# A ring of four places, and the tensor engine's steady state as a loop of two heads: one decode step of gated attention and SwiGLU

## The chip, the core and the metric

The kernel runs on one core of a Trainium2 chip. The metric is device time in microseconds (us) from the start of the program to its end. The kernel before takes 2550.09 us (median of 3 runs, 2549.92 to 2551.15).

The engines have short names in the profile: PE is the tensor engine (PEld its weight loads), DVE the vector engine, ACT the scalar engine, POOL the general engine, and SP the engine that only issues DMAs here. An engine's name with a q behind it (SPq) is its sequencer: it waits or issues while the engine itself computes nothing.

## What is computed

One token `x` (1 x 512) is mixed from an attention branch and an MLP branch:

```python
# H, Sk, Dh = 32, 65536, 128; all inputs bf16
g = sigmoid((x * gate_w).sum())
q = (x @ wq).reshape(H, Dh)
scores = einsum("hd,hkd->hk", q, k_cache) * Dh ** -0.5
o = einsum("hk,hkd->hd", softmax(scores), v_cache)
a = o.reshape(H * Dh) @ wo
b = (silu(x @ w_gate) * (x @ w_up)) @ w_down        # w_gate, w_up: 512 x 1792
out = g * a + (1 - g) * b
```

Each head has 16 MB of keys and 16 MB of values, so the two caches together are 1.07 GB that are read once. Everything else is small: `wq` and `wo` are 4 MB each, the three MLP weights 1.75 MB each.

## The kernel before

**Stream.** SP issues all large reads in one fixed order, made by `plan_stream` (L25 to L50). A read brings 32 KB to each of the 128 partitions, 4 MB in all; a head has four reads of keys and four of values, written here K(h,t) and V(h,t). The order is: `wq`, K(0,0), `wg`, `wu`, `wd`, then the rest of the keys of heads 0 and 1, and from head 2 on K(h,t) and V(h-2,t) by turns. Values trail keys by two heads, and the last eight reads are values, with `wo` ahead of the last head's. The very last read is cut into pieces of 2, 1 and 1 MB.

**Ring.** The reads land in `ring`, 160 KB per partition, as 20 slots of 8 KB (L78 to L97). A normal read takes four slots, so there are five places. `wq` has the first, K(0,0) the second, `wg` and `wu` share the third, `wd` has the fourth with a gap behind it, and K(0,1) the fifth. Before a read is issued SP waits until the former owner of its slots is used up (L219 to L229): `s_q` for `wq` (the query projection has run), `s_h` for `wg` and `wu` (the MLP's first products have run), `s_b` for `wd`, `ktdone` for keys (transposed by DVE), `pvdone` for values (multiplied by PE). SP issues in order, so a wait also holds back all later reads.

**Keys.** DVE transposes a place of keys in two units of 2 MB into `kt`, which has two buffers (L361 to L367, `kt[:, i % 2]`); the second waits for PE to have finished with the unit two before (`qkdone`). PE then runs 16 matmuls of 512 columns per unit (L459), which lay the scores of a head over one bank of PSUM, `psS`. After a head's eighth unit DVE takes the maximum, POOL reduces it over the partitions, ACT takes the exponential with a running sum, and DVE turns the probabilities into `pb`.

**Values.** PE multiplies a place of values in four half units (L473 to L482), 32 matmuls of 512 columns in all, into `psO`. ACT scales a finished head by the inverse of its sum (`row_norm`), and PE's `turn` (L428) transposes the row with 4 small matmuls into a column of `psT`. Head 31 is done otherwise: 128 matmuls of one column per place (L485). When the second place of head 31 is done, PE waits for `wo` and runs `project` for heads 0 to 30 (L492 to L495), 31 matmuls of 512 columns; `project(31)` follows after the last values. DVE casts the 31 columns of `psT` at once before that (L380).

**MLP.** It is folded into the start. PE runs `mlp_up` after the fourth unit of keys of head 0 (the second half of K(0,1)) and `mlp_down` after the fifth. On DVE `mlp_steps` stands behind the transpose of the fifth unit.

PE's whole program is written out, 9118 matmuls with 9118 weight loads.

## Time and profile before

| what | value |
|---|---|
| median of 3 runs | 2550.09 us |
| profiled execution | 2550.52 us |
| its span (first to last instruction) | 2548.7 us |
| mean granted clock of PE | 0.917 |
| read from HBM | 1087.64 MB, 427 GB/s over the span |
| busy: PE, DVE, ACT, POOL | 2052.2, 1168.9, 54.4, 25.9 us |
| one transpose of a key unit (L367) | 4426 ns |
| 4 MB of keys or values, from issue to landing (median) | 37.8 and 39.7 us |

The span is 1.8 us shorter than the time of the same execution; that rest lies ahead of and behind the program's instructions. Busy times are of one profiled execution. Matmuls are pipelined and their ends are modelled, so PE's busy share says little by itself. The time from issue to landing holds the wait behind the reads issued earlier, since all share one queue. A line number in the profile is a line of the kernel before.

### The profile page before, as it was taken

How to read it: one execution, taken by the hardware profiler on the slowest of the kernel's cores; microseconds unless marked ns; L12 is line 12 of the kernel's file. 1: busy time of each engine (PE TensorE's matmuls, PEld its weight loads, DVE VectorE, ACT ScalarE, POOL GpSimd, SP SyncE). 2: the span in 40 equal slices, each digit the busy share in tenths (PEclk: the TensorE clock that was granted, in tenths of full speed). 3: DMA queues.
4: the chain of work that ended last, by engine and by line, in shares of the span. 5: the costliest groups of instructions: out<-in, count | busy, mean ns of one | idle time of the engine just before them, and what ended most of it. 6: DMA issues, size and time to landing. Idle time of an engine off the chain costs nothing.

```text
span 2548.7 us, 19566 instructions
## 1 busy us (share of the span) xinstructions
PE 2052.2 (81%) x9118; PEld 812.3 (32%) x9118; DVE 1168.9 (46%) x374; ACT 54.4 (2%) x162; POOL 25.9 (1%) x75
## 2 busy tenths in 40 slices
PE   3888788878888888788778878887888888878886
PEld 2333233333333333233333333332333333333333
DVE  4754544454444444544454444445444544454420
ACT  0000000000000000000000000000000000000000
POOL 0000000000000000000000000000000000000000
PEclk8899999999998999998999998999999899899896
DMA  9999999999999999999999999999999999999998
GB/s 415 401 429 433 430 431 431 432 430 432 428 434 430 434 429 432 430 432 430 431 430 432 430 432 430 432 431 430 432 430 433 429 433 430 431 431 431 432 424 330
DMA packets 41927, 1088.90 MB, mean 427 GB/s; under 512 B 4211, under 2 KB 8310, under 8 KB 8310
## 3 DMA queue, kind: packets, MB, share of 16 engines
q1 hardware_dynamic: 41844, 1087.65, 99.4%
q8 instruction: 71, 1.16, 0.2%
q14 instruction: 10, 0.08, 0.0%
q10 hardware_dynamic: 2, 0.00, 0.0%
HBM read 1087.64 MB, written 0.00 MB: 427 GB/s over the span
## 4 chain that ended last, share of the span: by engine, by line
DMA 59%; PE 27%; DVE 10%; issue 3%; SPq 0%; DVEq 0%
DMA ring<-in_A_k_cache_dram 57%; PE psS L459 13%; PE psO L478 13%; DVE kt L367 10%; DMA ring<-in_A_v_cache_dram 3%; PE psO L485 0%; PE psY L439 0%; PE psT L433 0%; PE psM L416 0%; DVE mxs L349 0%; PE psY L424 0%; SPq L240 0%; DVE brow L345 0%; DVE gwrow L386 0%; DVE pb L355 0%
## 5 line engine op out<-in xcount | busy, mean ns | idle before, releaser
L367 DVE STREAM_TRANSPOSE kt<-ring 128x4096 uint32<-128x4096 uint32 x256 | 1125.4, 4426 | 1254.7 <-DMA ring<-in_A_k_cache_dram 1251.6
L459 PE MATMUL psS<-kt,qw 128*128 128x512 bf16 x4096 | 1110.2, 433 | 453.4 <-DVE kt L367 453.4
L478 PE MATMUL psO<-ring,pb 128*4 128x512 bf16 x3968 | 883.7, 380 | 7.0 <-DMA ring<-in_A_v_cache_dram 7.0
L459 PEld LDWEIGHTS psS<-kt,qw 128*128 128x128 bf16 x4096 | 419.6, 106 | 1142.0 <-DVE kt L367 537.6
L478 PEld LDWEIGHTS psO<-ring,pb 128*4 128x4 bf16 x3968 | 333.3, 87 | 535.3 <-issue 56.3
L290 ACT ACTIVATE nbias<-amx 128x1 f32<-128x1 f32 x32 | 6.5, 203 | 2338.7 <-POOL amx L261 2338.7
L261 POOL PARTITION_ALL_REDUCE amx<-mxs x32 | 11.3, 353 | 2384.5 <-DVE mxs L349 2384.5
L433 PEld LDWEIGHTS psT<-unit,orow 4*128 4x128 f32 x248 | 30.7, 190 | 13.1 <-issue 13.0
L433 PE MATMUL psT<-unit,orow 4*128 4x1 f32 x248 | 33.3, 251 | 0.0
L485 PE MATMUL psO<-pb,ring 128*128 128x1 bf16 x512 | 14.2, 165 | 19.2 <-DMA ring<-in_A_v_cache_dram 18.2
L380 DVE CAST oTn<-psT 128x31 bf16<-128x31 f32 x1 | 0.2, 195 | 61.8 <-PE psT L433 61.8
L355 DVE STREAM_TRANSPOSE pb<-pa 128x512 bf16<-128x512 bf16 x32 | 21.4, 670 | 6.4 <-PE psO L478 6.4
L349 DVE TENSOR_REDUCE mxs<-psS 128x1 f32<-128x512 f32 x32 | 20.9, 653 | 4.8 <-PE psS L459 4.8
L294 ACT ACTIVATE pa<-psS,nbias 128x512 bf16<-128x512 f32 x32 | 22.0, 687 | 1.0
L275 ACT ACTIVATE orow<-psO,Li 4x512 f32<-4x512 f32 x31 | 20.9, 674 | 42.3 <-PE psO L478 37.4
L485 PEld LDWEIGHTS psO<-pb,ring 128*128 128x128 bf16 x512 | 13.9, 102 | 20.2 <-issue 14.1
L263 POOL PARTITION_ALL_REDUCE Lt<-rsum x32 | 12.3, 386 | 36.4 <-ACT pa L294 36.4
L395 PE MATMUL psM<-ones,xrow 1*128 1x1 bf16 x4 | 0.3, 173 | 13.2 <-DMA gwrow<-in_gate_w_dram 13.2
L439 PE MATMUL psY<-ring,oTn 128*1 128x512 bf16 x32 | 10.0, 480 | 0.4 <-DVE oTn L383 0.4
L383 DVE TENSOR_SCALAR oTn<-psO,Li 128x1 bf16<-128x1 f32 x1 | 0.2, 221 | 19.7 <-PE psO L485 19.7
L280 ACT COPY qw<-qd 128x16 bf16<-128x16 bf16 x32 | 7.9, 252 | 6.0 <-DVE qd L333 6.0
L416 PEld LDWEIGHTS psM<-xTb,ring 128*128 128x128 bf16 x112 | 6.9, 159 | 0.2
(39 smaller groups left out, 42.8 us busy)
## 6 DMA issues: line engine op xcount, KB each, us to landing
ring<-in_A_k_cache_dram SPq DMA_DIRECT2D x128, 4096.0 KB, 37.8
ring<-in_A_v_cache_dram SPq DMA_DIRECT2D x127, 4096.0 KB, 39.7
ring<-in_A_wq_dram SPq DMA_DIRECT2D x1, 4096.0 KB, 12.2
ring<-in_A_wo_dram SPq DMA_DIRECT2D x1, 4096.0 KB, 40.3
ring<-in_A_v_cache_dram SPq DMA_DIRECT2D x1, 2048.0 KB, 38.8
ring<-in_A_v_cache_dram SPq DMA_DIRECT2D x2, 1024.0 KB, 40.0
ring<-in_B_w_gate_dram SPq DMA_DIRECT2D x1, 1792.0 KB, 26.2
ring<-in_B_w_up_dram SPq DMA_DIRECT2D x1, 1792.0 KB, 30.0
```

The lines of the kernel that those rows point to most:

```text
L261: nc.gpsimd.partition_all_reduce(amx[:, h:h + 1], mxs[:, h:h + 1], P, RMAX).then_inc(s_ar, 1)
L263: nc.gpsimd.partition_all_reduce(Lt[:, h:h + 1], rsum[:, h:h + 1], P, RADD).then_inc(s_L, 1)
L275: nc.scalar.mul(orow[0:4, :], psO[0:4, h % 2, :], Li[0:4, h:h + 1]).then_inc(s_or, 1)
L294: nc.scalar.activation(pa[:, h % 2, :], psS[:, h % 2, :], ACT.Exp, bias=nbias[:, h:h + 1], scale=SCALE, accum_out=rsum[:, h:h + 1]).then_i ...
L349: nc.vector.reduce_max(mxs[:, h:h + 1], psS[:, h % 2, :], AX_X).then_inc(s_mx, 1)
L355: nc.vector.transpose(pb[:, h % 2, :], pa[:, h % 2, :]).then_inc(s_pb, 1)
L367: nc.vector.transpose(o, src).then_inc(ktdone, 1)
L433: last = nc.tensor.matmul(psT[:, h:h + 1], orow[0:4, i * Dh:(i + 1) * Dh], unit[0:4, i:i + 1], start=(i == 0), stop=(i == 3))
L439: last = nc.tensor.matmul(psY[0:1, :], oTn[:, h:h + 1], wo_ap[:, h, :], start=(h == 0), stop=(h == H - 1))
L459: last = nc.tensor.matmul(psS[:, h % 2, :], qw[:, h % 2, je, at0:at0 + 128], ktb[i % 2][:, je // 2, k, :, je % 2], start=(u == 0 and k == ...
L478: last = nc.tensor.matmul(psO[0:4, h % 2, :], pbk[:, h % 2, col // 16, col % 16:col % 16 + 4], vt[:, r * Dh:(r + 4) * Dh], start=(col == 0 ...
L485: last = nc.tensor.matmul(psO[:, h % 2, 0:1], vt[:, r * Dh:(r + 1) * Dh], pbk[:, h % 2, col // 16, col % 16:col % 16 + 1], start=(col == 0 ...
```

## The change

PE's program, the ring and the place of `wo` are rewritten; the arithmetic and the order of the matmuls of the steady state stay.

- The ring has four places of 32 KB per partition instead of five. Item n of the stream always goes to place n mod 4, so the 16 reads of two heads meet the same addresses in every round.
- `wo` leaves the ring. It is read into `kt`, the two buffers of transposed keys, after the values of head 30, once all matmuls on keys are done.
- On PE the steady state becomes a loop. Ahead of it stand the first 20 items written out; the loop's body holds 16 items (two heads); `(240 - 20) // 16` gives 13 rounds; the last 12 items are written out again. Inside the loop every wait compares a semaphore with a constant plus the loop's register `more`, which grows by 16 a round. So that each semaphore grows by 16 a round, several steps now add `STEP = 8`.
- `turn` uses two columns of `psT` by turns instead of one per head, and so ACT copies each head's column into `oTn` (`column`), and `turn` waits for the copy two heads before. DVE's cast of all columns goes.
- `turn` moves from behind the first quarter of a head's second place of values to its end. `project` for heads 0 to 30 moves from behind the second place of head 31 to behind the third. A place of values is waited for once instead of four times.

```diff
-RING = 20
+NPL = 4
+STEP = 8
...
+    for n, item in enumerate(items):
+        s = n % NPL
...
+        owner[s] = item
+        if item == ("v", H - 2, PL - 1):
+            landed["wo"] = len(dmas)
+            dmas.append((("wo",), 0, 0, None, None))
...
-        ring = sb("ring", [P, RING * HU], BF16)
+        ring = sb("ring", [P, NPL, PLACE], BF16)
...
+        wo_ap = kt[:].rearrange("p b t -> p (b t)").bitcast(BF16).rearrange("p (h n) -> p h n", h=H)
...
+            for n, (item, r0, r1, s, old) in enumerate(dmas):
+                name = item[0]
+                if old is not None and r0 == 0:
+                    if old[0] == "k":
+                        sp.wait_ge(ktdone, 2 * (old[1] * PL + old[2]) + 2)
+                    elif old[0] == "v":
+                        sp.wait_ge(pvdone, old[1] * PL + old[2] + 1)
                     else:
-                        need[key[0]] = 1
+                        sp.wait_ge({"wq": s_q, "wg": s_h, "wd": s_b}[old[0]], 1)
...
+                elif name == "wo":
+                    sp.wait_ge(qkdone, UN * H)
...
+            def column(h):
+                act.wait_ge(s_pt, h + 1)
+                nc.scalar.copy(oTn[:, h:h + 1], psT[:, h % 2:h % 2 + 1]).then_inc(s_oc, STEP)
...
+            def turn(h, more=0):
+                pe.wait_ge(s_or, STEP * (h + 1) + more)
+                if h >= 2:
+                    pe.wait_ge(s_oc, STEP * (h - 1) + more)
...
+            def run(item, more=0):
+                kind, h, t = item
+                if kind == "k":
+                    scores(h, t, more)
+                else:
+                    values(h, t, more)
+                    if t == 1 and h >= 1:
+                        turn(h - 1, more)
...
+            head, per = 4 + 4 * PL, 4 * PL
+            loops = (len(steady) - head) // per
+            for item in first:
+                if item[0] == "k":
+                    run(item)
+            for item in steady[:head]:
+                run(item)
+            with pe.Fori(0, STEP * 2 * loops, STEP * 2) as more:
+                for item in steady[head:head + per]:
+                    run(item, more)
+            for item in steady[head + per * loops:]:
+                run(item)
+            for item in last:
+                run(item)
+                if item == ("v", H - 1, PL - 2):
+                    arrived(pe, landed["wo"])
+                    for h in range(H - 1):
+                        project(h)
             project(H - 1)
```

## Prediction

> **What bounds it now.** I read the page first (DMA row, queues, chain, costliest groups), then SP's own issues in time, then the stages by windows, then PE's last 40 us.

> ```profile
> DMA  9999999999999999999999999999999999999998
> ...
> q1 hardware_dynamic: 41844, 1087.65, 99.4%
> q8 instruction: 71, 1.16, 0.2%
> ...
> DMA 59%; PE 27%; DVE 10%; issue 3%; SPq 0%; DVEq 0%
> ...
> L367 DVE STREAM_TRANSPOSE kt<-ring 128x4096 uint32<-128x4096 uint32 x256 | 1125.4, 4426 | 1254.7 <-DMA ring<-in_A_k_cache_dram 1251.6
> L459 PE MATMUL psS<-kt,qw 128*128 128x512 bf16 x4096 | 1110.2, 433 | 453.4 <-DVE kt L367 453.4
> ```

> The 16 DMA engines are full in all slices, DVE idles for keys, and PE idles for DVE. So the time is bytes at a fixed rate, plus stretches in which the engines have nothing queued, plus what follows the last byte. In the steady state two key transposes start like this:

> ```profile
> 1271.96 8.77 DVE L367 STREAM_TRANSPOSE kt<-ring 128x4096 uint32<-128x4096 uint32 x2 [10.66 <-DMA ring<-in_A_k_cache_dram]
> 1291.39 4.45 DVE L367 STREAM_TRANSPOSE kt<-ring 128x4096 uint32<-128x4096 uint32 x1 [10.66 <-DMA ring<-in_A_k_cache_dram]
> ```

> Both start on a landing, and between them lie one read of keys and one of values: 19.43 us, so 9.71 us for each 4 MB. One stretch of nothing queued shows in the windows of the start (columns: stretch, length, PE, PEld, DVE, ACT, POOL busy, clock, DMA share, GB/s):

> ```profile
> 60.00:64.00 4.00, 4.00 (x65) 3.79 (x63) 1.45 (x1) 0.00 (x0) 0.00 (x0) 1.00 0.95 406
> 64.00:66.00 2.00, 2.00 (x36) 2.00 (x36) 0.00 (x0) 0.00 (x0) 0.00 (x0) 0.87 0.04 16
> 66.00:68.00 2.00, 2.00 (x23) 1.44 (x23) 0.50 (x3) 0.18 (x1) 0.00 (x0) 0.50 0.00 0
> 68.00:72.00 4.00, 4.00 (x11) 1.32 (x10) 0.26 (x2) 0.00 (x0) 0.00 (x0) 0.50 1.09 393
> ```

> SP's waits (us in total, times, longest) and its issue, from the timeline:

> ```profile
> SPq L229 <- PE psM L416: 33.9, 1, 33.9
> ```

> ```profile
> 67.27 0.33 SPq L240 DMA_DIRECT2D ring<-in_A_k_cache_dram  x1
> ```

> The read issued at 67.27 is K(1,0). It waited 33.9 us for `s_h`, since it takes the place of `wg` and `wu`; the reads ahead of it were through near 66 and the queue stood empty about 2.5 us. The end:

> ```profile
> 2522.76 1.01 PE L485 MATMUL psO<-pb,ring 128*128 128x1 bf16 x32 [6.07 <-DMA ring<-in_A_v_cache_dram]
> ...
> 2525.49 2.72 PE L485 MATMUL psO<-pb,ring 128*128 128x1 bf16 x96
> 2528.14 9.39 PE L439 MATMUL psY<-ring,oTn 128*1 128x512 bf16 x31
> 2537.47 4.21 PE L485 MATMUL psO<-pb,ring 128*128 128x1 bf16 x159
> 2542.68 2.75 PE L485 MATMUL psO<-pb,ring 128*128 128x1 bf16 x97 [0.99 <-issue]
> ```

> V(31,1) lands at 2522.7. Two more reads at 9.71 put V(31,2) near 2532.5 and the last piece near 2542.3 (the windows show the engines run dry there). PE ends at 2545.43, the span 3.3 us later.

> **Part 1, the ring at the start: +9.7.** With four places `wq`, K(0,0), `wg`+`wu` and `wd` hold all of them, and each later read shifts one owner back. K(0,1) now waits for `s_q` (17.8, when SP issued K(0,2) before), K(0,2) for K(0,0)'s transposes (32.9): both come while earlier reads still run, so they cost nothing; uncovered they would cost 18 and 33 us. K(0,3), issued before at 32.96, now takes the place of `wg`+`wu` and waits for `s_h`. That can't come earlier: `mlp_up` stands behind the second half of K(0,1), which lands at 46.75 in both. So K(0,3) goes out at 67.27, when K(1,0) did, and every read behind it lands one read later. The queue runs dry at 66 - 9.7 = 56.3 and stands until 68.2: 12 us instead of 2.5. The next wait, K(1,0)'s for `s_b`, ends at 76.42, as K(1,1)'s did before, about 1 us ahead of the end of K(0,3)'s bytes (68.2 + 9.7). DVE and PE lose nothing, because unit 6 of the keys, the first half of K(0,3), is transposed only at 81.7, held up by `mlp_steps`. But nothing gives the DMA time back: **+9.71**, bounds 9.4 and 10.

> **Part 2, the ring in the steady state: 0.** A place of values lands at 1281.67 (1271.96 + 9.71), PE is done with it at 1292.45 (1285.38 + 7.07), and SP's next read goes out at 1292.49: 10.8 us after the landing, 12 where `turn` lies between. Keys take 8.8 (two transposes). With four places three reads, 29.1 us, are still queued at a landing, so 17 us of slack cover the release; with five it was 27. If that cover were gone each us would count.

> **Part 3, the loop's back-edge: 0 on the path, 13 times.** It falls between a `turn` and a K item, where PE idles 3.65 us for DVE. No branch is in the trace; bounds for the stall are 1.0 us (the one idle for "issue", 2542) and 12 us (the 1 KB read of `x`, issued at 1.15 behind a full queue, was waited for until 13.18). Even 12 leaves PE 8.4 late, inside 17. I take 0; the visible stall is the nearer row. [...]

> **Part 4, waits on a register: 0.** The body has 36 (16 `ktdone`, 8 arrivals, 12 others). PE idles for DVE 406.1 us in 140 to 2400, 28 us per round of 16 reads (155.4 us). At the largest regular "issue" gap between weight loads, 0.44 us, 36 cost 16: covered. At nothing, the dropped value waits are a small gain, off the path as well.

> **Part 5, instruction reads: +1.8.** 71 packets for 18311 PE records make 256 instructions each, and 0.2% of the span is 5.1 us, 0.07 a packet. They come all along the run, one per 36 us. A body is 8 x 128 + 32 + 36 to 72, so 4.3 packets. If it stays loaded, 12 x 4.3 packets go: -3.6. If each round reads it anew with two cut or unused blocks, 26 come on top: +1.8. The stall of 0.99 in PE's densest stretch says that little is held ahead, so I take +1.8; doubled traffic, +5.1, is the upper end.

> **Part 6, the end: +3.85.** `project` for 31 heads moves behind V(31,2). Let L be the last landing (2542.5 at most; PE's end is L + 2.93). V(31,2) lands at L - 9.8; its 128 matmuls take 3.55 (row at 2513.14), `project` 9.39, the last place's 128 another 3.5: L + 6.8 with three 0.05 steps, 3.85 later than now. The pieces land during `project`, so PE, not DMA, sets the end. All instructions of `project` count; nothing else is queued behind it but the last values. The 9.39 is 11 matmuls at 0.43 (granted clock 0.50 until 2532) and 20 at 0.21. Bounds: all 31 fast, 6.6, gives +1.0; another stall of 1 us +4.9. [...] The row shows it slow, so I keep 9.39.

> **Without weight.** `wo` in `kt` is gated by matmuls on keys (done at 2456), while SP reaches it behind V(30,3) at 2463: 0; if that wait ended last, V(31,0) and all behind would be late. ACT's 31 copies at 0.25 us lie in an engine 2% busy, wanted two heads on; uncovered 7.8 us. `turn`'s later place and its wait for a copy one head old hold up only values behind it: 0. DVE's dropped cast: 0.

> **Sum.** Profiled execution 2550.52 + 9.71 + 3.85 + 1.8 = 2565.9. The median of the runs is 0.4 lower: **2565.5**.

> **Rivals.** (a) *PE becomes the bound*: 36 waits and one branch cost over 28 us a round, that is 0.78 us per wait. For it: no register wait is in the trace. Against: 0.44 is the largest such gap. At 1 us each, 8 x 13 = 104 us more: 2670. (b) *Not slower: reads get faster.* With three to four reads outstanding instead of four to five, 4 MB might take less than 9.71. From 9.65 on, 256 reads give 15.4 us back and the time is 2550 or less. Against: the engines are at share 1.00 and 431 GB/s in both 140:1200 and 1200:2400, and a queue only needs to be non-empty. (c) *The loop spares its reads and the end runs warm*: 9.4 + 1.0 - 3.6, about 2557, still slower.

> **Chances.** Forecast with its bounds 0.82; (a) 0.07; (b) 0.05; (c) 0.06. Lower bound 2557 from (c); upper 2572 from 10 + 4.9 + 5.1 = 20 above 2550.09, plus 2 for late places after a back-edge; (a) and (b) lie outside. A measurement of this kernel can tell 0.2%, 5.1 us, from no change: slower needs 2555.2. Case (b) is split between same 0.03 and faster 0.02; the rest is slower, 0.95.

> **What would show it.** Right: DMA share near 0 from 56 to 68, SP's `s_h` wait ending with a read at 67.3 that is the eighth large one instead of the ninth; 9.71 us per read after; L439 x31 starting behind V(31,2), and last byte to span's end 9.5 to 11 us instead of 6.3; q8 at 80 to 110 packets. Wrong: PE idling for "issue" by tens of us a round, a DMA share below 0.99 in the middle, or another duration per read.

## The result and the profile after

The changed kernel takes 2555.00 us (median of 20 runs, 2553.04 to 2556.97); the kernel before takes 2550.55 us (20 runs, 2549.56 to 2551.66) in the same comparison. The ratio is 1.0018, with a 95% interval of 1.0011 to 1.0025: slower by 4.5 us, just under the 0.2% that the prediction put as its bound for "slower". The forecast of 2565.5 us is 10.5 us too high, and its range, 2557 to 2572, misses the time by 2 us. The profiled execution took 2555.05 us, its span 2553.3.

The page of the changed kernel, the rows that answer to those shown before:

```profile
DMA  8999999999999999999999999999999999999998
...
q1 hardware_dynamic: 41844, 1087.65, 99.2%
q8 instruction: 22, 0.36, 0.1%
...
DMA 75%; DVE 12%; issue 10%; PE 2%; SPq 0%; DVEq 0%
...
L326 DVE STREAM_TRANSPOSE kt<-ring 128x4096 uint32<-128x4096 uint32 x256 | 1125.6, 4426 | 1255.5 <-DMA ring<-in_A_k_cache_dram 1252.6
L396 PE MATMUL psS<-kt,qw 128*128 128x512 bf16 x3970 | 1104.3, 442 | 463.8 <-DVE kt L326 463.2
```

The first slice of the DMA row has lost a tenth; the rest is as full as before. The instruction queue q8 has 22 packets where it had 71. PE's idle time for DVE is 463 us, as good as the 453 before (some matmul records are missing in this trace).

The start, by windows of the changed kernel (columns as before: PE, PEld, DVE, ACT, POOL busy, clock, DMA share, GB/s):

```profile
52.00:56.00 4.00, 4.00 (x14) 1.49 (x13) 3.14 (x1) 0.00 (x0) 0.00 (x0) 0.69 0.44 188
56.00:60.00 4.00, 3.94 (x22) 1.84 (x21) 3.56 (x1) 0.00 (x0) 0.00 (x0) 1.00 0.02 4
60.00:64.00 4.00, 4.00 (x70) 4.00 (x69) 0.89 (x1) 0.00 (x0) 0.00 (x0) 1.00 0.00 0
64.00:68.00 4.00, 3.75 (x47) 3.04 (x48) 0.76 (x4) 0.18 (x1) 0.00 (x0) 0.59 0.39 106
```

SP's longest wait there, and the issue that ends it, which is now K(0,3):

```profile
SPq L190 <- PE psM L373: 33.7, 1, 33.7
```

```profile
66.65 0.33 SPq L190 DMA_DIRECT2D ring<-in_A_k_cache_dram  x1
```

PE at the end:

```profile
2523.70 3.57 PE L423 MATMUL psO<-pb,ring 128*128 128x1 bf16 x128 [6.07 <-DMA ring<-in_A_v_cache_dram]
2527.21 1.86 PE L434 MATMUL psT<-unit,orow 4*128 4x1 f32 x8
2533.43 3.57 PE L423 MATMUL psO<-pb,ring 128*128 128x1 bf16 x128 [4.36 <-DMA ring<-in_A_v_cache_dram]
2536.93 9.73 PE L443 MATMUL psY<-kt,oTn 128*1 128x512 bf16 x31
2546.59 3.37 PE L423 MATMUL psO<-pb,ring 128*128 128x1 bf16 x128
```

`project` stands between V(31,2) and V(31,3), and the last place's 128 matmuls begin 3.4 us after the last landing (2543.16), without a wait. From the landings in the two traces the 4.5 us come apart:

| stretch | before, us | after, us | difference | predicted |
|---|---|---|---|---|
| start, to K(1,0)'s landing | 80.46 | 89.96 | +9.50 | +9.71 |
| K(1,0)'s landing to the last landing (same reads) | 2462.04 | 2453.20 | -8.84 | +1.8 |
| last landing to the end of the span | 6.23 | 10.11 | +3.88 | +3.85 |
| span | 2548.73 | 2553.27 | +4.54 | +15.4 |

Start and end came about as worked out. The middle gained 9 us that were forecast as a small loss.

### The profile page after: what moved, and what is told of

It is laid out like the page before. It is cut to its first block, busy times and chain, and to the rows that moved or that the text cites. A ratio compares the mean times of both kernels' runs of the same rounds, so it can differ in the third digit from the quotient of the medians.

```text
span 2553.3 us, 19880 instructions
## 1 busy us (share of the span) xinstructions
PE 2042.0 (80%) x8992; PEld 824.2 (32%) x9118; DVE 1168.7 (46%) x373; ACT 56.1 (2%) x193; POOL 26.0 (1%) x75
## 3 DMA queue, kind: packets, MB, share of 16 engines
q1 hardware_dynamic: 41844, 1087.65, 99.2%
## 4 chain that ended last, share of the span: by engine, by line
DMA 75%; DVE 12%; issue 10%; PE 2%; SPq 0%; DVEq 0%
DMA ring<-in_A_k_cache_dram 72%; DVE kt L326 12%; DMA ring<-in_A_v_cache_dram 3%; PE psS L396 1%; DMA gwrow<-in_gate_w_dram 0%; PE psY L443 0%; SPq L190 0%; PE psO L418 0%; PE psO L423 0%; PE psM L373 0%; PE psM L358 0%; PE psY L381 0%; DVE orow L276 0%; DVE brow L301 0%; DVE fin L343 0%
## 5 line engine op out<-in xcount | busy, mean ns | idle before, releaser
L326 DVE STREAM_TRANSPOSE kt<-ring 128x4096 uint32<-128x4096 uint32 x256 | 1125.6, 4426 | 1255.5 <-DMA ring<-in_A_k_cache_dram 1252.6
L396 PEld LDWEIGHTS psS<-kt,qw 128*128 128x128 bf16 x4096 | 429.7, 108 | 1124.3 <-issue 388.4
L423 PEld LDWEIGHTS psO<-pb,ring 128*128 128x128 bf16 x512 | 13.8, 102 | 26.0 <-issue 15.4
L443 PE MATMUL psY<-kt,oTn 128*1 128x512 bf16 x32 | 10.3, 492 | 0.4 <-DVE oTn L340 0.4
L373 PE MATMUL psM<-xTb,ring 128*128 128x1 bf16 x112 | 6.8, 198 | 0.0
```

Of the source, the lines that this page charges most:

```text
L326: nc.vector.transpose(o, src).then_inc(ktdone, 1)
L373: done = nc.tensor.matmul(psM[:, o + j:o + j + 1], w[:, c, :, j], xTb[:, c:c + 1], start=(c == 0), stop=(c == Dc - 1))
L396: done = nc.tensor.matmul(psS[:, h % 2, :], qw[:, h % 2, je, at0:at0 + 128], ktb[i % 2][:, je // 2, k, :, je % 2], start=(u == 0 and k == ...
L423: done = nc.tensor.matmul(psO[:, h % 2, 0:1], v[:, (r + j) * Dh:(r + j + 1) * Dh], pbk[:, h % 2, k, rho + j:rho + j + 1], start=(t == 0 an ...
```

## Experiments

The question was where the 9 us of the middle come from. Theory A: the loop's code stays loaded, so 49 instruction packets fall away, and a packet costs the stream of reads more than the 0.07 us of the prediction. Rival B: the smaller ring, with fewer reads outstanding, makes each read faster. Rival C: the packets go, but at 0.07 each they give only 3.4 us, and something else gives the rest. The other runs test the start and the end by mending each alone. All medians are of 5 to 11 runs; the kernel before had 2550.8 us beside them (15 runs).

### The loop written out again

```diff
-            loops = (len(steady) - head) // per
+            loops = 0
...
-            with pe.Fori(0, STEP * 2 * loops, STEP * 2) as more:
-                for item in steady[head:head + per]:
-                    run(item, more)
```

> The changed kernel with PE's loop written out again; the ring of four places, the end and the MLP's place stay. Theory A (the loop's body stays loaded, and the instruction reads that fall away are what the reads of the caches gain in the middle): about 71 instruction packets again instead of 22, and the 8.8 us that the stretch from K(1,0)'s landing to the last landing lost come back, so about 2564 us, near the sum of the prediction without its part 5. Rival B (the gain in the middle comes from the ring: fewer reads outstanding make each faster): packets rise, the time stays at 2555 us. Rival C (packets cost 0.07 us each, as the prediction priced them): 49 x 0.07 = 3.4 us, 2558.5 us.

Measured: 2563.56 us, ratio to before 1.0050 (1.0036 to 1.0063). The queues on its page:

```profile
q8 instruction: 71, 1.16, 0.2%
```

The 71 packets are back, and so are 8.6 us (2563.56 - 2555.00), with the ring of four still there. B falls, and so does C. K(1,0) to the last landing takes 2462.96 us, as in the kernel before. The prediction without its part 5 would have been 2563.7 for this kernel.

### Six rounds of the loop

```diff
-            loops = (len(steady) - head) // per
+            loops = 6
```

> The changed kernel with 6 rounds of the loop instead of 13, the other 7 rounds written out. Theory A: each round written out brings 4.2 packets back, so 22 + 30 = 52 packets, and 7/13 of what the fully written out form costs: with 8.8 us for all, 2555 + 4.9 = 2560 us, packets absent only in the middle of the run. Rival B: 2555. Rival C: 2557.

Measured: 2560.50 us, 51 packets. 29 of the 49 packets bring back 5.5 of the 8.6 us, near A's 2560; C's 2557 lies below all of this kernel's runs (2558.82 to 2560.95).

### A loop body of four heads

```diff
-            head, per = 4 + 4 * PL, 4 * PL
+            head, per = 4 + 4 * PL, 8 * PL
...
-            with pe.Fori(0, STEP * 2 * loops, STEP * 2) as more:
+            with pe.Fori(0, STEP * 4 * loops, STEP * 4) as more:
```

> The changed kernel with a loop body of four heads, some 2150 PE instructions or 8.4 packets of 256, and 6 rounds. Theory A1 (PE's instruction store holds 8 packets or fewer, and the body of two heads stayed because it has 4.2): every round reads its body anew, 70 packets or more, the time goes back to 2563 or 2564 us, and each of the 5 jumps back waits for a packet, which the queue of reads hides. Theory A2 (the store holds more): 71 - 5 x 8.4 = 29 packets and 2555 + 7 x 0.18 = 2556 us. In both the price per packet is the 0.18 us that the fully and the half written out loop gave.

Measured: 2564.08 us, 80 packets: A1. The rows of the loop's own line show the difference. In the changed kernel (body 1076 instructions by the records between two branches, in which 8 matmuls are missing; columns: least, median, largest ns):

```profile
L466 PEldq COMPARE_BRANCH  x13: 76/207/231, 480.0 to 2345.3; - x13
```

and with the body of four heads (2146 records, 16 matmuls missing), with PE's idle time from its waits:

```profile
L466 PEldq COMPARE_BRANCH  x6: 79/6510/7004, 636.3 to 2200.1; - x6
```

```profile
PE psS L396 <- issue: 15.8, 5, 4.4
```

A jump back took 0.21 us in the changed kernel, whose body is still loaded, and 5.9 to 7.0 us here, where it has to be read. Even then the matmuls already handed to PE ran on (17 of them start behind the branch, in its first 3.2 us), so PE idled 3.2 us a jump, and the ring hid that: the time is 0.5 us over the form written out, no more than its nine extra packets would cost. This kernel has the loop and its waits on a register, and not the gain: the gain goes with the packets, not with the loop as such.

### The MLP's steps earlier

```diff
+            def mlp_row():
                 dve.wait_ge(s_b, 1)
...
+                    if i == 1:
+                        mlp_steps()
                     if i == 4:
-                        mlp_steps()
+                        mlp_row()
...
-                    if h == 0 and u == 3:
+                    if h == 0 and u == 1:
                         mlp_up()
-                    if h == 0 and u == 4:
+                    if h == 0 and u == 2:
                         mlp_down()
```

`mlp_row` is the last step of `mlp_steps`, which waits for `s_b`.

> The changed kernel with mlp_up behind the second key unit instead of the fourth, mlp_down behind the third, and DVE's MLP steps behind the second (the last of them behind the fifth). If the lost time at the start is K(0,3)'s wait for the MLP's first products, that wait ends near 46 us instead of 66.6, the queue never runs dry, K(0,3) lands at 65.8 instead of 80.0, and all later landings move by 14.2 to 14.5: 2540.5 us. If a ring of four is short at the start for another reason (key transposes, the query projection), the queue still runs dry and less than half of that comes.

Measured: 2540.81 us, ratio to before 0.9962 (0.9949 to 0.9976). The windows where the changed kernel's engines stood empty:

```profile
52.00:56.00 4.00, 4.00 (x13) 1.44 (x12) 3.37 (x1) 0.00 (x0) 0.00 (x0) 0.61 0.97 418
56.00:60.00 4.00, 4.00 (x19) 1.33 (x18) 3.12 (x1) 0.00 (x0) 0.00 (x0) 1.00 0.93 401
60.00:64.00 4.00, 4.00 (x19) 1.74 (x18) 2.20 (x3) 0.00 (x0) 0.00 (x0) 1.00 1.09 467
```

K(0,3) goes out at 43.92 and lands at 66.00, K(1,0) at 75.75. The whole loss at the start hangs on the place of the MLP's steps, which SP's wait for `s_h` follows.

### The same in the kernel before

The same moves in the kernel with the ring of five, written out.

> The kernel before, ring of five and all written out, with the MLP's steps as early as in the changed kernel's variant. Its own empty stretch at 66 to 68 should go, so K(1,0) lands at 75.8 instead of 80.46: 2550.5 - 4.6 = 2546 us. If ring size matters only at the start, this equals the changed kernel written out (2563.6) with the start mended (-14.4) and the end moved back (-3.85): 2545.3. If a fifth place is worth something in the steady state as well, it comes out below that by more than 1.5 us.

Measured: 2545.33 us, ratio 0.9979 (0.9970 to 0.9988). That is the value added up for a ring of four that is mended at both ends and written out: 2545.3 by the expected differences, 2545.8 by the measured ones (-14.2 and -3.6). That kernel itself was not run. So once the start is mended no worth of a fifth place above 1 us shows.

### `project` moved back

```diff
-                if item == ("v", H - 1, PL - 2):
+                if item == ("v", H - 1, PL - 3):
                     arrived(pe, landed["wo"])
```

> The changed kernel with project for heads 0 to 30 moved back behind the second place of head 31. By the prediction's part 6 it costs 3.85 us where it stands: 2551.2 us, PE's end 3 us behind the last landing instead of 6.8. If the end is set by something else (the wait for wo in kt, the column copies), the time stays at 2555.

Measured: 2551.39 us (11 runs), 3.6 less than the changed kernel. Its profile ends otherwise than expected: PE is done with the last values 1.06 us behind the last landing and not 3, with `project` at 8.13 us instead of 9.39 and without the stall of 0.99 us ahead of the last values.

### Loop, early MLP and an early `project`

```diff
-                if item == ("v", H - 1, PL - 2):
+                if item == ("v", H - 1, 0):
                     arrived(pe, landed["wo"])
-                    for h in range(H - 1):
+                    for h in range(H - 2):
                         project(h)
+                if item == ("v", H - 1, 1):
+                    project(H - 2)
```

with the early MLP steps as above, and `project` of heads 0 to 29 waiting for 30 columns.

> The changed kernel with the early MLP steps, and with project for heads 0 to 29 behind the first place of head 31 and for head 30 behind the second. Start as in the early variant (2540.8). At the end nothing but the last 32 rows is left for PE after the last landing, so PE ends 1 us behind it instead of 6.8: 2540.8 - 5.8 = 2535 us. If PE falls behind at the end (31 slow matmuls ahead of the second place's values), 2537 to 2541.

Measured: 2535.97 us (2535.93 to 2536.20), ratio to before 0.9942 (0.9928 to 0.9955): it beats both kernels. PE's last rows:

```profile
2504.17 8.87 PE L447 MATMUL psY<-kt,oTn 128*1 128x512 bf16 x30
2512.97 3.40 PE L427 MATMUL psO<-pb,ring 128*128 128x1 bf16 x128
...
2520.02 3.57 PE L427 MATMUL psO<-pb,ring 128*128 128x1 bf16 x128 [0.96 <-DMA ring<-in_A_v_cache_dram]
...
2529.83 1.01 PE L427 MATMUL psO<-pb,ring 128*128 128x1 bf16 x32 [1.45 <-DMA ring<-in_A_v_cache_dram]
```

PE waits for each of the last landings again, and is done with the last values 1 us behind the last.

## Why the prediction was wrong, point by point

**The step that failed is part 5, the instruction reads: +1.8 forecast, -8.84 measured.** It failed twice.

First, which case. The prediction named the case that came (the body stays loaded) and gave it as the lower end; it took the other. In the changed kernel q8 has no packet between 456 us, ahead of the first jump back, and 2360 us, behind the last. The reason given, that the 0.99 us idle for "issue" at the end shows little held ahead, says nothing about code already passed: the loop needs what lies behind PE, not what lies ahead. The rows of the loop's own line show both cases: the body of some 1080 instructions (4.2 packets) jumped back in 0.21 us without a read, and the one of some 2150, with 80 packets in all, was read anew each round and jumped back in 5.9 to 7.0 us.

Second, the price. The prediction divided a packet's time by 16 engines, 0.07 us. Over nine profiles the stretch from K(1,0) to the last landing goes with the packets:

| packets of q8 | kernels | stretch, us |
|---|---|---|
| 22 | changed; early MLP; `project` back; loop, start and end | 2453.20, 2454.10, 2454.69, 2453.95 |
| 51 | six rounds | 2458.51 |
| 71 | before; written out; before with early MLP | 2462.04, 2462.96, 2461.77 |
| 80 | body of four heads | 2463.66 |

From 22 to 71 the means differ by 8.27 us, 0.17 a packet; at that slope 51 packets should give 2458.9 and 80 should give 2463.8. One packet takes 0.93 to 1.26 us of one engine in the trace of before. The landings of that trace step by 1.2 to 1.4 and by 0.2 to 0.5 us about once each in 300 us, that is in 8 packets; in the kernel before with the early MLP it is one step of 1.4 to 1.65 in 8.

So the cost does not spread evenly. A read raises its semaphore in 16 single steps, one for each part of it, and it has landed with the last; the trace has the time of each (4208 for the 263 large reads of the kernel before). In the kernel before with the early MLP the last of the 16 stood 0.09 us behind the 15th in the read that landed at 289.8, and 1.43 us behind it at 301.0, after the packet at 297.7. At 339.8, after the next packet, a second part had joined it (0.12 us). Each further packet made one more part late, until at 592.4 eight stood within 0.5 us, and the packet at 596.8 moved the last one again.

Per packet one part falls back by 1.5 us (median, in this kernel as in the kernel before), and the packets go round eight of the 16 parts: in the kernel before all 16 lay within 2.1 us at 323.9, and at 2442.4 eight lay within 0.6 us of the landing and the other eight were 7.8 to 13.2 us ahead. A packet thus costs the landings 1.5 / 8 = 0.19 us, near the slope of 0.17; the prediction had a packet's own time over 16. Why one part loses 1.5 us to a packet of 0.93 to 1.26 stays open, and the trace names no engine.

The step stood in the view that the prediction quoted, one row ahead of the two that it shows. DVE's timeline of before:

```profile
1252.53 8.77 DVE L367 STREAM_TRANSPOSE kt<-ring 128x4096 uint32<-128x4096 uint32 x2 [11.83 <-DMA ring<-in_A_k_cache_dram]
```

DVE waited 11.83 us there and 10.66 at the next two. Taking two even landings as the cadence hid 1.2 us in every 300.

With the right price the lower end of part 5 would have been 52 x 0.17 = -8.8, and the sum 2550.1 + 9.7 + 3.85 - 8.8 = 2554.8.

**Right, by its own steps:** part 1 (+9.50 for +9.71, and up to +10.9 in the other profiles with this start, where K(1,0) lands as late as 91.32; the wait, its end at 66.65, and the eighth large read behind it; the early MLP takes it away); part 2 (no cost of the ring in the steady state above 1 us, by the loop written out and by the ring of five with the mended start); part 3 (0 on the path, though its bounds were for a stall that came only with four heads in the body); part 4 (waits on a register move nothing that shows: the loop of four heads has them too and lies on the line of the packets); part 6 (+3.88 for +3.85, and 3.6 when undone). That part 6 agrees to 0.03 us is luck. In the five profiles with `project` behind V(31,2) the span ends 8.4 to 10.1 us after the last landing, in the three with it behind V(31,1) 4.4 to 6.2; only the means, 9.3 and 5.4, differ by 3.9.

On the clock in part 6 the row held. In all nine profiles the granted clock was still 0.50 when `project` began behind 3.5 to 5.4 us of one-column work, and rose to 1.00 only 2.6 to 5.9 us later. In the kernel before it stood at 0.50 from 2506.0 to 2533.3, through the one-column matmuls of V(31,0) (3.55 us at 2513.14) and the 5.4 us of one-column work from 2522.76 on. At its start it fell from 1.00 to 0.50, at 65.5, while `mlp_up`'s 112 one-column matmuls ran (60.35 to 67.18). So in that trace one-column work did not raise the clock, and under `mlp_up` the clock fell.

**Rivals.** (a), PE as the bound, did not come. (b), faster reads, came in its effect but not by its cause: the reads of the middle gained 8.8 us, and none of it shows as the ring's. (c) combined spared reads with a warm end, that is `project` at a granted clock of 1.00 throughout; the first half came, at more than twice its price; the second did not: `project` took 9.73 us and not the estimated 6.6.

## What to carry to other kernels

Here the DMA engines stood at share 1.00 in the middle of the run (460 to 2340), and with the loop whose body stayed loaded, and 22 packets of instructions for 71, the stretch from K(1,0) to the last landing was 8.3 us shorter. So where reads fill the DMA engines, count the packets, and price them by the part of a read that they make late (0.19 us each here, 0.17 by the slope), not by their mean share (0.07). When a ring loses a place, follow the first round of owners, where the weights sit: here K(0,3) took the place of `wg` and `wu` from K(1,0) and waited until 66.65 for a product, and the start took 9.5 us longer, while the steady state showed no cost above 1 us. For work that is moved at the end, count what it puts between the last landing and the last matmul: `project` behind V(31,2) put 3.9 us there.
